# Spacing layer norm, a deeper ring of hidden tiles, phi written into the exp buffers, and a last block replicated on the matmul engine

## The chip, the cores and the metric

The kernel runs on one core of one Trainium2 chip. The metric is device time in microseconds (us) of that core, read as the median of several executions. Each execution also reports the mean granted clock of the matmul engine (1.00 is full speed), and one execution of each kernel was profiled. Engines are named as in the profile: PE (matmul; PEld is its weight load), ACT (ScalarE), DVE (VectorE), POOL (GpSimd), SP (which issues most of the DMAs).

## The reference

A transformer block in parallel form: the output is `x + attention(xn) + mlp(xn)`, with `xn = layernorm(x)`. There are 2048 tokens of width 512, 32 heads of 16, all bf16. Attention runs in four segments of 512 tokens. Each segment has causal softmax attention of its own, and reads a memory `M`, `z` that the segments before it have summed up.

```python
xn = _layernorm(x)
# attention, for each segment s of 512 tokens, each head (q, k, v = xn @ wq, wk, wv)
phi = lambda t: jnp.where(t > 0, t + 1.0, jnp.exp(t))
p = softmax(qs @ ks.T * scale + causal_mask)
a_dot = p @ vs
a_mem = (phi(qs) @ M) / (phi(qs) @ z + 1e-06)
o = g * a_mem + (1 - g) * a_dot          # g = sigmoid(beta), one number for each head
M = M + phi(ks).T @ vs
z = z + phi(ks).sum(0)
# ... all segments' o put together
return x + o @ wo + silu(xn @ w1) @ w2   # w1: 512 x 1792, w2: 1792 x 512
```

## The kernel before

The kernel keeps a feature-by-token layout. In each segment there are four blocks (`dt` 0 to 3) of eight heads, and each block has five score tiles of 128 x 2048. That makes 4 x 4 x 5 = 80 score tiles, and each is followed by one exp on ACT. These 80 exps are the beat of the program. All other work (projections, the MLP's 56 tiles of `w1` output, `w2`, `wo`, the memory) is cut into pieces that a small scheduler in the build places between score tiles. It keeps a virtual clock; `later(ns, fn)` emits `fn` once that clock has moved on by `ns`. The clock decides only the **order** of the instructions on each engine. The engines then run their lists in order and wait on semaphores.

Layer norm of a coming segment is done ahead, on DVE, in the gaps:

```python
HRING = 17                                     # w1 outputs that may wait for w2
ppool = ctx.enter_context(tc.tile_pool(name="ppool", bufs=8))      # Pt: exp outputs
hpool = ctx.enter_context(tc.tile_pool(name="hpool", bufs=HRING))  # hT: w1 outputs
work  = ctx.enter_context(tc.tile_pool(name="work",  bufs=2))

def ln_async(s):
    def step(j):                               # normalize tile j, transpose it by DMA
        xn_t = ln_norm(s, j)
        def move():
            nc.sync.dma_start_transpose(xnT[s][:, :, j * P : (j + 1) * P], xn_t[:])
            # ...
        later(700, move)
        if j < TPS - 1:
            later(1000, lambda: step(j + 1))
    def stats(half):                           # two tiles of statistics at once
        ln_stats(s, 2 * half)
        ln_stats(s, 2 * half + 1)
        ln_rstd(s, half)
        later(1500, lambda: stats(1) if half == 0 else free())
    # ... free() waits for the segment before last, then step(0)
    stats(0)

# where score tiles are emitted:
if (s, dt) == (0, 0):
    later(9000, lambda: ln_async(1))
elif dt == 1 and s + 2 < NSEG:
    ln_async(s + 2)
```

`phi(t)` is made as `max(t, 0) + min(exp(t), 1)`, with the exp on ACT, the min on POOL and the rest on DVE. For the keys the result goes to a tile `phiKT` (two buffers), and a DMA transposes it into `phiK`:

```python
def phi_part(src, dst, after, acc=None):
    ek = work.tile([P, L], BF16, name="ek")                    # two buffers
    nc.scalar.activation(out=ek[:], in_=src, func=AF.Exp)
    # ... mn() on POOL: ek = min(ek, 1); 800 ns later:
    def fin():
        nc.vector.scalar_tensor_tensor(out=dst, in0=src, scalar=0.0, in1=ek[:],
                                       op0=ALU.max, op1=ALU.add, accum_out=acc)
```

A `w1` tile is four matmuls on PE, a tanh on ACT, and a DVE pass that makes `hT`. At most `HRING` of them may be waiting for `w2`:

```python
while s not in ln_done or hcount["made"] - hcount["freed"] >= HRING:
    yield False
ps = gemm4(...)                                # 4 matmuls of 512 columns
nc.scalar.activation(out=th[:], in_=ps[:, :], func=AF.Tanh, scale=0.5)
# 700 ns later on DVE: hT = (th + 1) * ps
```

At the end of a segment, DVE takes the reciprocal of the softmax sums and of the memory's denominators. The result goes to DRAM and comes back broadcast, so that each head's number stands on its 16 partitions (`oT` and `Dr` hold it first, then are scaled in place):

```python
def scale(dt):
    nc.vector.tensor_tensor(out=oT[:, dt, :], in0=st["N_sb"][dt][:], in1=oT[:, dt, :], op=ALU.mult)
    if s > 0:
        nc.vector.tensor_tensor(out=Dr[:, dt, :], in0=st["phiQT"][:, dt, :], in1=Dr[:, dt, :], op=ALU.mult)
    later(1500, lambda: fin(dt))               # fin: psN = Mbf x Dr on PE, oT += psN on DVE
# ...
later((6500 if s < NSEG - 1 else 3000) + 1000 * (dt - d0), lambda dt=dt: scale(dt))
```

And the end of the program, after the last exp:

```python
for j in range(TPS):
    for ft in range(FA, FT):
        w2_part(st, j, psOs[j][:, :], range(ft, ft + 1), None)   # 28 w2 matmuls
        for g in list(due):
            pull(g)                            # norm_fill of the last segment
while st["normed"] < DT:
    ...
for j in range(TPS):
    wo_part(s, st, j, psOs[j][:, :])           # 16 wo matmuls, four for each j
```

The softmax here doesn't subtract the row's maximum and nothing guards it: scores larger than these inputs give would overflow.

## Time and profile before

| | before |
|---|---|
| median | 278.85 us (278.35 to 279.17, 4 runs) |
| profiled run: span from first to last instruction | 278.4 us |
| mean granted PE clock in that run | 0.969 |
| start of the first exp / start of the last exp | 14.3 us / 251.3 us |
| mean distance between exps | 3.0 us, for an exp of 1.88 us |

First, from the page of the kernel before: busy microseconds of each engine with the share of the span and the number of instructions; the clock granted to PE in 40 equal slices, in tenths of full speed; and the chain of work that ended last, by engine.

```profile
PE 235.1 (84%) x1908; PEld 100.7 (36%) x1908; DVE 170.5 (61%) x297; ACT 206.6 (74%) x192; POOL 127.9 (46%) x223
PEclk9999968999999997997999999999999999999979
PE 40%; DVE 22%; ACT 19%; issue 10%; POOL 4%; DMA 3%; ACTq 0%; DVEq 0%; SPq 0%
```

PE is the busiest engine and has the largest part of the chain, but only 40% of it. The chain changes hands all the time. A total says little in such a program; one has to ask, stretch by stretch, who is last.

The stretches used below are made from the exps. **Interval n** runs from the start of exp n to the start of exp n+1 (n counts from 0; read from ACT's timeline). The **tail** runs from the start of the last exp to the end. The next view, windows of the kernel before, gives five such stretches: intervals 5 and 6, 12 to 17, 24 to 36, 70 to 72, and the first 23.5 us of the tail. The columns are named in its first line; "x" counts instructions.

```profile
core 0: us, PE busy (x) PEld busy (x) DVE busy (x) ACT busy (x) POOL busy (x), PEclk, DMA share, GB/s
29.88:41.11 11.23, 5.90 (x56) 2.08 (x55) 11.02 (x25) 6.21 (x9) 7.37 (x16) 0.79 0.38 57
54.71:73.06 18.35, 15.64 (x127) 6.45 (x126) 13.73 (x22) 15.98 (x15) 13.60 (x21) 1.00 0.13 28
89.83:133.43 43.60, 34.14 (x290) 14.14 (x289) 30.18 (x53) 32.95 (x31) 28.25 (x45) 0.92 0.17 43
224.78:235.83 11.05, 7.18 (x70) 2.68 (x69) 9.39 (x19) 7.72 (x8) 2.91 (x5) 1.00 0.02 6
251.27:274.77 23.50, 19.03 (x104) 7.74 (x102) 14.17 (x24) 4.64 (x6) 1.64 (x2) 0.93 0.13 39
```

In the first line DVE is busy 11.02 of 11.23 us, while PE has 5.90 us of work: DVE alone sets that stretch, though it is the third engine by total. In the tail PE works 19.03 of 23.50 us, with a clock below 1.

DVE's timeline of the kernel before, from a little ahead of that first stretch, shows what fills it. (Left out between two statistics is the 0.18 us pass that gathers them.) Columns: start, duration, engine, line, operation, output and inputs, number; in brackets the idle time before, and what ended it.

```profile
24.68 0.66 DVE L134 BATCH_NORM_STATS2 stats<-x_sb 128x6 f32<-128x512 bf16 x1
...
28.71 0.69 DVE L226 SCALAR_TENSOR_TENSOR phiKT<-kT,ek 128x512 bf16<-128x512 bf16 x1 [3.15 <-DMA phiK<-phiKT]
...
29.33 0.69 DVE L134 BATCH_NORM_STATS2 stats<-x_sb 128x6 f32<-128x512 bf16 x1
...
30.15 0.66 DVE L134 BATCH_NORM_STATS2 stats<-x_sb 128x6 f32<-128x512 bf16 x1
...
30.95 0.66 DVE L302 CAST qT<-ps 128x512 bf16<-128x512 f32 x1
31.52 0.68 DVE L349 SCALAR_TENSOR_TENSOR hT<-th,ps 128x512 bf16<-128x512 bf16 x1
```

DVE stands idle for 3.15 us because `phiKT` has two buffers and the transposing DMA has not freed one. Then statistics come in pairs, and `qT` and `hT`, which PE and ACT need, stand behind them.

PE's timeline at the end of the kernel before:

```profile
264.30 4.05 PE L473 MATMUL psOt<-w_sb,hT 128*128 128x512 bf16 x11 [2.26 <-DVE hT L349]
...
268.57 2.56 PE L473 MATMUL psOt<-w_sb,hT 128*128 128x512 bf16 x11
270.96 0.38 PE L434 MATMUL psN<-Dr,Mbf 128*128 128x512 bf16 x1
271.18 3.93 PE L500 MATMUL psOt<-wo_sb,oT 128*128 128x512 bf16 x16
```

And DVE's in the same place:

```profile
261.51 1.75 DVE L667 RECIPROCAL rec<-zf 128x256 f32<-128x256 bf16 x1
263.29 0.35 DVE L668 TENSOR_SCALAR recg<-rec,gcol 128x256 bf16<-128x256 f32 x1
...
270.48 0.43 DVE L426 TENSOR_TENSOR Dr<-phiQT,Dr 128x512 bf16<-128x512 bf16 x1 [0.38 <-DMA Dr<-rec_d]
```

From the end of `recg` at 263.64 to the start of the last product with `Dr` at 270.48 it takes 6.84 us: one DMA to DRAM, two back. Only then can the last block's `psN` run, and all 16 `wo` matmuls come after it. Eleven `w2` matmuls take 4.05 us here, and eleven later ones 2.56 us: the first group started after an idle time of 2.26 us and ran at about half the clock.

### The profile page before, as it was taken

To read this page: it belongs to the slowest core of one execution; us is meant where nothing else is said; L and a number is where in the kernel's file an instruction comes from. 1 tells how busy PE (TensorE), PEld (TensorE's weight loads), DVE (VectorE), ACT (ScalarE), POOL (GpSimd) and SP (SyncE) were. 2 spreads that over 40 slices of the span, in tenths; PEclk is the share of its full clock that TensorE was granted. 3 is DMA by queue.
4 is the path that set the end of the run, shared out by engine and by line. 5 is a ranking of instruction groups with operands and counts; after the bars stand their busy time and mean duration, and the time that the engine had idled before them with its cause. 6 is when DMAs were issued, how large, how long until landed. Compare 5 with 4: busy or idle time off the path is not lost.

```text
span 278.4 us, 5105 instructions
## 1 busy us (share of the span) xinstructions
PE 235.1 (84%) x1908; PEld 100.7 (36%) x1908; DVE 170.5 (61%) x297; ACT 206.6 (74%) x192; POOL 127.9 (46%) x223
## 2 busy tenths in 40 slices
PE   7589569996989759796999988999999876998595
PEld 7433124432333333242344442343334322343241
DVE  4664895488656945974354749973436367457624
ACT  1499669888999887776799996887898986682300
POOL 3654653485724387585233555573343223423000
PEclk9999968999999997997999999999999999999979
DMA  6999141010112220103000440000100400131112
GB/s 210 380 358 221 38 62 29 3 30 19 28 22 51 48 77 12 38 11 76 26 26 11 86 154 11 8 5 27 62 13 17 144 13 14 45 117 34 33 49 75
DMA packets 29285, 18.69 MB, mean 67 GB/s; under 512 B 15180, under 2 KB 28748, under 8 KB 29260
## 3 DMA queue, kind: packets, MB, share of 16 engines
q1 hardware_dynamic: 29228, 18.35, 23.7%
q8 instruction: 15, 0.25, 0.3%
q14 instruction: 10, 0.08, 0.1%
q10 hardware_dynamic: 32, 0.01, 0.0%
HBM read 11.53 MB, written 2.49 MB: 50 GB/s over the span
## 4 chain that ended last, share of the span: by engine, by line
PE 40%; DVE 22%; ACT 19%; issue 10%; POOL 4%; DMA 3%; ACTq 0%; DVEq 0%; SPq 0%
ACT Pt L562 13%; PE ps L209 12%; PE psA L473 7%; PE psS L554 6%; DVE hT L349 5%; PE psO L473 5%; ACT th L343 4%; DVE stats L134 3%; PE psPV L629 3%; DVE rec L667 2%; PE psOt L473 2%; PE psO L500 2%; DMA phiK<-phiKT 2%; POOL Pt L574 2%; DVE phiKT L226 2%
## 5 line engine op out<-in xcount | busy, mean ns | idle before, releaser
L562 ACT ACTIVATE Pt<-psS 128x2048 bf16<-128x2048 f32 x80 | 150.3, 1879 | 20.8 <-PE psS L554 18.5
L574 POOL TENSOR_SCALAR_AFFINE_SELECT Pt<-Pt 128x512 bf16<-128x512 bf16 (+1 forms) x112 | 78.9, 718 | 97.6 <-ACT Pt L562 97.5
L209 PE MATMUL ps<-xnT,w_sb 128*128 128x512 bf16 x224 | 56.9, 388 | 5.3 <-DVE hT L349 3.2
L349 DVE SCALAR_TENSOR_TENSOR hT<-th,ps 128x512 bf16<-128x512 bf16 x56 | 37.3, 681 | 36.2 <-ACT th L343 35.7
L343 ACT ACTIVATE th<-ps 128x512 bf16<-128x512 f32 x56 | 32.6, 612 | 6.6 <-DVE hT L349 5.3
L209 PEld LDWEIGHTS <-w_sb 128*128 128x128 bf16 x224 | 20.6, 99 | 31.7 <-issue 13.0
L473 PEld LDWEIGHTS <-hT 128*128 128x128 bf16 x224 | 20.4, 100 | 32.2 <-issue 10.1
L473 PE MATMUL psA<-w_sb,hT 128*128 128x512 bf16 x112 | 28.9, 380 | 0.0
L554 PE MATMUL psS<-qT,kTo 32*128 32x512 bf16 (+3 forms) x256 | 17.6, 305 | 9.0 <-ACT Pt L562 7.7
L473 PE MATMUL psO<-w_sb,hT 128*128 128x512 bf16 x84 | 22.6, 395 | 0.0
L554 PE MATMUL psS<-qT,kT 16*128 16x512 bf16 (+3 forms) x256 | 17.6, 305 | 5.5 <-ACT Pt L562 5.3
L220 POOL TENSOR_SCALAR ek<-ek 128x512 bf16<-128x512 bf16 x24 | 16.1, 675 | 6.5 <-ACT ek L217 6.4
L509 DVE SCALAR_TENSOR_TENSOR o_t<-psO,acc 128x512 bf16<-128x512 f32 x12 | 8.3, 689 | 15.2 <-PE psO L500 15.1
L554 PEld LDWEIGHTS <-kTo 32*128 32x128 bf16 x256 | 6.7, 91 | 29.8 <-issue 28.4
L209 PE MATMUL ps<-xnT,wk_sb 128*128 128x512 bf16 x60 | 17.2, 390 | 0.1
L640 ACT CAST N_sb<-psPV 128x512 bf16<-128x512 f32 x16 | 9.4, 588 | 10.3 <-PE psPV L629 5.5
L209 PE MATMUL ps<-wv_sb,xnT 128*128 128x512 bf16 x64 | 15.8, 380 | 1.2 <-DVE V_109 L308 1.2
L209 PE MATMUL ps<-xnT,wq_sb 128*128 128x512 bf16 x60 | 16.8, 397 | 0.0
L488 DVE SCALAR_TENSOR_TENSOR acc<-psA,x_sb 128x512 f32<-128x512 f32 x16 | 11.0, 689 | 8.1 <-PE psA L473 8.1
L302 DVE CAST qT<-ps 128x512 bf16<-128x512 f32 x16 | 11.0, 685 | 7.1 <-PE ps L209 6.4
L629 PE MATMUL psPV<-Pt,V_109 128*32 128x512 bf16 (+3 forms) x256 | 11.1, 311 | 4.8 <-DVE hT L349 3.7
L638 DVE CAST No_t<-psPV 128x512 bf16<-128x512 f32 x16 | 11.0, 687 | 6.1 <-PE psPV L629 6.1
(82 smaller groups left out, 278.5 us busy)
## 6 DMA issues: line engine op xcount, KB each, us to landing
w_sb<-in_B_w_dram SPq DMA_DIRECT2D x2, 1792.0 KB
oT<-rec_d SPq DMA_DIRECT2D x16, 128.0 KB
out_dram<-o_t SPq DMA_DIRECT2D x12, 128.0 KB
Dr<-rec_d SPq DMA_DIRECT2D x12, 128.0 KB
x_sb<-in_A_x_dram SPq DMA_DIRECT2D x1, 1024.0 KB
N_sb<-No_t SPq DMA_DIRECT2D x64, 16.0 KB
x_sb<-in_A_x_dram SPq DMA_DIRECT2D x2, 256.0 KB
wk_sb<-in_A_wk_dram SPq DMA_DIRECT2D x1, 512.0 KB
```

What stands on the lines that cost most here:

```text
L209: nc.tensor.matmul(ps[:, :], lhsT=lhsTs(ki), rhs=rhss(ki), start=(ki == 0), stop=(ki == DT - 1))
L220: nc.gpsimd.tensor_scalar(out=ek[:], in0=ek[:], scalar1=1.0, scalar2=0.0, op0=ALU.min, op1=ALU.max)
L302: nc.vector.tensor_copy(out=qT[:], in_=ps[:, :])
L343: nc.scalar.activation(out=th[:], in_=ps[:, :], func=AF.Tanh, scale=0.5)
L349: nc.vector.scalar_tensor_tensor(out=hT[:], in0=th[:], scalar=1.0, in1=ps[:, :], op0=ALU.add, op1=ALU.mult)
L473: nc.tensor.matmul(psO, lhsT=st["hT"][ft][:, j * P : (j + 1) * P], rhs=w2_sb[:, ft, :], start=(ft in (0, FA)), stop=(ft == last),)
L488: nc.vector.scalar_tensor_tensor(out=acc[:], in0=psA[:, :], scalar=0.5, in1=x_sb[:, s * TPS + j, :], op0=ALU.mult, op1=ALU.add,)
L554: nc.tensor.matmul(psS[:, g, c : c + nq], lhsT=kk[r0:r1, kt * P : (kt + 1) * P], rhs=st["qT"][dt][r0:r1, kt * P : L], start=True, stop=Tru ...
L562: nc.scalar.activation(out=Pt[:], in_=psS[:], func=AF.Exp, scale=SCALE)
L574: nc.gpsimd.affine_select(out=v, in_=v, compare_op=ALU.is_ge, fill=0.0, base=0, pattern=[[0, v.shape[1]], [1, P]], channel_multiplier=-1,)
L629: nc.tensor.matmul(psPV[32 * g : 32 * g + 32, kt * P : L], lhsT=V[:, kt, 4 * dt + g, par : par + 2, :].rearrange("p r d -> p (r d)"), rhs= ...
L638: nc.vector.tensor_copy(out=dst[:], in_=psPV[:, :])
```

## The change

The intent, in four parts:

1. **LN**: layer-norm statistics come one tile at a time, 2 us apart (before: pairs, 1.5 us apart); normalized tiles 2 us apart (before: 1 us); segment 1 starts 2 us earlier, segments 2 and 3 one block later.
2. **phi**: the keys' phi goes back into its exp buffer `ek` (a ring of four); `phiKT` is gone. Freed memory goes to part 3.
3. **Ring**: 21 `w1` outputs may wait instead of 17; `Pt` has 7 buffers instead of 8.
4. **Tail**: for the last block the reciprocals are replicated over partitions by four matmuls with a selector matrix, not through DRAM; `oT` and `Dr` read the result in PSUM. The `wo` matmuls of the first three blocks go ahead of the last block's. The sums of the last block are issued from SP's queue, not ACT's.

```diff
-HRING = 17
+HRING = 21
-    ppool = ... name="ppool", bufs=8
+    ppool = ... name="ppool", bufs=7
@@ ln_async
-            later(700, move)
+            later(900, move)
-                later(1000, lambda: step(j + 1))
+                later(2000, lambda: step(j + 1))
-        def stats(half):
-            ln_stats(s, 2 * half)
-            ln_stats(s, 2 * half + 1)
-            ln_rstd(s, half)
-            later(1500, lambda: stats(1) if half == 0 else free())
+        def stats(j):
+            ln_stats(s, j)
+            if j % 2:
+                ln_rstd(s, j // 2)
+            later(2000, lambda: stats(j + 1) if j < TPS - 1 else free())
@@ where score tiles are emitted
-                later(9000, lambda: ln_async(1))
-            elif dt == 1 and s + 2 < NSEG:
+                later(7000, lambda: ln_async(1))
+            elif dt == 2 and s + 2 < NSEG:
@@ phi_part, k_tile
-        ek = work.tile([P, L], BF16, name="ek")
+        ek = work.tile([P, L], BF16, name="ek", bufs=4)
-                out=dst, in0=src, ...
+                out=ek[:] if dst is None else dst, in0=src, ...
-            phiKT = work.tile([P, L], BF16, name="phiKT")
-            def k_transposes():
+            def k_transposes(phiKT):
@@ norm_fill
-        def scale(dt):                 # oT first, then Dr, both in place
+        def scale(dt, R, D):           # Dr first, then oT, from R and D
+            if s == NSEG - 1 and dt == DT - 1:
+                reps = []
+                for w in (1, 0):
+                    ps = pp.tile([P, L], F32, name="psRep", tag="ps")
+                    for b in range(2):
+                        nc.tensor.matmul(ps[:, 256 * b : 256 * b + 256],
+                            lhsT=sel3[:, b, w, :], rhs=rec_d[:], start=True, stop=True)
+                    reps.append(ps)
+                scale(dt, reps[1][:, :], reps[0][:, :])
+                continue
@@ wo_part: takes the blocks to do; end of the program:
-    while st["normed"] < DT: ...
-    for j in range(TPS):
-        wo_part(s, st, j, psOs[j][:, :])
+    for n in (DT - 1, DT):
+        while st["normed"] < n: ...
+        for j in range(TPS):
+            wo_part(s, st, j, psOs[j][:, :], range(DT - 1) if n < DT else range(DT - 1, DT))
@@ pv_part: sums on SP's queue; recip returns before the DRAM write for the last block
-        q_sum = nc.scalar if last and dt == DT - 1 else nc.sync
+            if last and dt == DT - 1:
+                st["rec"][dt] = (recg, clock["vt"] + 1500)
+                return
```

(The build of the selector `sel3` from the identity matrix, on POOL, is left out.)

More of the change, by code (lines that the diff above doesn't have):

```diff
@@ L57 @@
     segp = ctx.enter_context(tc.tile_pool(name="segp", bufs=2))
-    ppool = ctx.enter_context(tc.tile_pool(name="ppool", bufs=8))
+    ppool = ctx.enter_context(tc.tile_pool(name="ppool", bufs=7))
     hpool = ctx.enter_context(tc.tile_pool(name="hpool", bufs=HRING))
@@ L226, in fin @@
             nc.vector.scalar_tensor_tensor(
-                out=dst, in0=src, scalar=0.0, in1=ek[:], op0=ALU.max, op1=ALU.add, accum_out=acc
+                out=ek[:] if dst is None else dst, in0=src, scalar=0.0, in1=ek[:],
+                op0=ALU.max, op1=ALU.add, accum_out=acc,
             )
             if after is not None:
-                later(1000, after)
+                later(1000, lambda: after(ek))
         later(900, mn)
@@ L292, in k_tile @@
                 lambda: phi_part(
-                    kT[:], phiKT[:], k_transposes, st["zc"][:, dt : dt + 1]
+                    kT[:], None, k_transposes, st["zc"][:, dt : dt + 1]
                 ),
@@ L419, in norm_fill @@
         st["normed"] = 0
-        def scale(dt):
-            nc.vector.tensor_tensor(
-                out=oT[:, dt, :], in0=st["N_sb"][dt][:], in1=oT[:, dt, :], op=ALU.mult
-            )
+        def scale(dt, R, D):
             if s > 0:
                 nc.vector.tensor_tensor(
-                    out=Dr[:, dt, :], in0=st["phiQT"][:, dt, :], in1=Dr[:, dt, :], op=ALU.mult
+                    out=Dr[:, dt, :], in0=st["phiQT"][:, dt, :], in1=D, op=ALU.mult
                 )
+            nc.vector.tensor_tensor(
+                out=oT[:, dt, :], in0=st["N_sb"][dt][:], in1=R, op=ALU.mult
+            )
             later(1500, lambda: fin(dt))
@@ L454, in norm_fill @@
             rec_d = st["rec"][dt][0]
+            if s == NSEG - 1 and dt == DT - 1:
[3 more added lines that the diff above has]
+                    for b in range(2):
+                        nc.tensor.matmul(
+                            ps[:, 256 * b : 256 * b + 256], lhsT=sel3[:, b, w, :], rhs=rec_d[:],
+                            start=True, stop=True,
+                        )
+                    reps.append(ps)
+                scale(dt, reps[1][:, :], reps[0][:, :])
+                continue
             for w, dst in ((0, oT), (1, Dr))[:nw]:
@@ L462, in norm_fill @@
                 )
-            later((6500 if s < NSEG - 1 else 3000) + 1000 * (dt - d0), lambda dt=dt: scale(dt))
+            later((6500 if s < NSEG - 1 else 3000) + 1000 * (dt - d0), lambda dt=dt: scale(dt, oT[:, dt, :], Dr[:, dt, :]))
         while st["normed"] < DT:
@@ L495, in first_fill, with wo_part @@
         st["first_done"] = True
-    def wo_part(s, st, j, psO):
+    def wo_part(s, st, j, psO, dts=range(DT)):
         t = s * TPS + j
-        for dt in range(DT):
+        for dt in dts:
             nc.tensor.matmul(
@@ L504, in wo_part @@
             pe(215)
+        if dts[-1] < DT - 1:
+            return
         if s == NSEG - 1:
@@ L646, in sums @@
                     z0 = 16 * (1 - par)
-                    q_sum.dma_start(
+                    nc.sync.dma_start(
                         out=zf[r : r + 7 : 2, :],
@@ L671, in recip @@
             d0 = max(st["rec"], default=-1) + 1
+            if last and dt == DT - 1:
+                st["rec"][dt] = (recg, clock["vt"] + 1500)
+                return
             rec_d = dpool.tile([2, H, 2, 256], BF16, name="rec_d")
@@ L739 @@
     later(20000, gate)
+    sel3 = cpool.tile([P, 2, 2, P], BF16, name="sel3")
+    nc.gpsimd.tensor_copy(
+        out=sel3[:, :, :, :].rearrange("p b w (h d) -> p (b w) h d", d=DH),
+        in_=ident[:, :]
+        .rearrange("p (r h) -> p r h", r=4)[:, :, 24:32]
+        .unsqueeze(3)
+        .broadcast_to([P, 4, 8, DH]),
+    )
     bmask = cpool.tile([P, P], BF16, name="bmask")
@@ L874 @@
                 pull(g)
-    while st["normed"] < DT:
-        for g in list(due):
-            pull(g)
-        clock["vt"] += 200
-        run_due()
-    for j in range(TPS):
-        wo_part(s, st, j, psOs[j][:, :])
+    for n in (DT - 1, DT):
+        while st["normed"] < n:
+            for g in list(due):
+                pull(g)
+            clock["vt"] += 200
+            run_due()
+        for j in range(TPS):
+            wo_part(s, st, j, psOs[j][:, :], range(DT - 1) if n < DT else range(DT - 1, DT))
     clock["vt"] += 5000
```

## The prediction

> **What bounds the kernel now.** The busy table shows PE 235.1 of 278.4 us (84%), ACT 206.6, DVE 170.5; the chain of waits is PE 40%, DVE 22%, ACT 19%. No single engine bounds it. The 80 exps of score tiles (1.88 us each) start at 14.3 to 251.3 us, 3.0 us apart. For each interval I took the larger of PE's work (0.217 us per 512-column matmul) and ACT's (1.76 us per exp, 0.6 per other pass). This estimate sums to 213 us against 237 measured; most intervals match within 0.2 us. The excess sits in few places (timeline):
> - 29.9 to 41.1 us: two intervals of 5.9 and 5.3 us, 5.3 too long. DVE waited 3.1 us for a transpose to free a phiK buffer, then did layer-norm statistics (0.66+0.18 us each) in pairs while hT evictions, and PE, stood behind.
> - 57 to 68: ACT waits for DVE to free exp buffers, 1.7.
> - 89.8 to 133.4: 43.6 us for 13 intervals, about 9 too long. Statistics delay hT; the w1 ring is full, so PE has 0.9 to 1.1 us of work in two intervals; then its clock is half (matmuls at 0.43 us) as the projections start; an exp waits 1.4 us for a buffer.
> - 168 to 176 and 225 to 233: attention scaling on DVE, 5.5.
> - After the last exp (ends 253.2): 25.2 us. The sums go out on ACT's queue, delaying N's copy by 1.5 us; the reciprocal ends at 263.3; the round trip through DRAM lets Dr's product finish only at 270.9; PE's clock halves from 264.3 to 268.3; all 16 wo matmuls follow (271.2 to 275.1).
>
> **What the change does** (instruction order compared).
> 1. Layer norm: no work removed; statistics come one at a time, 2 us apart; segments 2 and 3 start a block later. phi goes back into the exp buffer (ring of 4), so DVE no longer waits for the first transposes. Segment 3's statistics and norms (3.2+1.6 us) fall into its projection burst, where DVE has about 21 us of work in 19 us: part is given back.
> 2. Ring 21: sixteen more w1 matmuls run where PE was empty; one nearly empty interval remains instead of two; two w1 tiles instead of four are left for the tail.
> 3. Seven Pt buffers: PV frees the oldest in time; about 0.
> 4. Tail: one rec write and two broadcasts vanish (263.7 to 270.5); four 256-column matmuls come in. Dr and oT read PSUM: 0.42 becomes 0.69 us, as other PSUM passes here; the Trainium skill, "VectorE: DVE Perf Modes", "Why PSUM operands drop a tier", agrees. 12 wo matmuls run before the last block is ready. PE's work becomes the limit (estimate 15 us after PV); sums wait behind earlier broadcasts, so the reciprocal gains about 1 us.
>
> **On the critical path (estimates):** startup -4; phi buffers -1.5; 90 to 133 us -3.5; 225 to 233 us -1; elsewhere -0.5; tail -2.5. Sum -13.
>
> **Predicted: 266.0 us, 80% range 261 to 272.** Faster by over 2%: 0.88; within 2%: 0.11; slower: 0.01.
>
> **Right or wrong in the profile:** the two long startup intervals fall to about 3.5 each, DVE's 3.1 us wait gone; the 13 intervals take about 40 us; no exp waits over 1 us for a phi buffer; last exp to end about 22.5 us, 12 wo matmuls before the last oT.
>
> **What would make it wrong:** exp buffers waiting for transposes, stalling ACT; DVE's burst in segment 1 costing more; PE idling before the replication, its clock halving anyway (0.217 to 0.43 us after gaps here).

## The result and the profile after

| | before | after |
|---|---|---|
| median | 278.85 us (278.35 to 279.17, 4 runs) | 271.14 us (270.24 to 272.39, 4 runs) |
| profiled span | 278.4 us | 270.7 us |
| mean granted clock in the profiled run | 0.969 | 0.974 |

The ratio is 0.9728, with a 95% interval of 0.9676 to 0.978: faster. Ratios here are the mean time of one kernel's fast runs over the mean of the other's fast runs of the same rounds, so they are not quite the ratio of the medians quoted. Executions over 1.5% slower than the fastest of the same kernel are left out of the means.

The four runs after are not alike: 272.39 us at clock 0.974, 272.02 at 0.981, 270.24 and 270.26 at 0.993. The same program is granted a different clock from run to run, and the profiled run is the slowest of the four. So differences below 1 us between two profiles are not to be leaned on.

From the page of the changed kernel, the same three lines:

```profile
PE 229.3 (85%) x1879; PEld 100.9 (37%) x1912; DVE 170.9 (63%) x297; ACT 206.0 (76%) x192; POOL 128.5 (47%) x224
PEclk9869999999999999999999999999999995999999
PE 39%; ACT 22%; DVE 18%; issue 11%; POOL 5%; DMA 3%; DVEq 0%; SPq 0%; ACTq 0%; POOLq 0%
```

The work is the same (DVE 170.5 to 170.9 us, ACT 206.6 to 206.0). What fell is time in which the last engine was waited for. New marks stand in the clock: a 5 in a slice near 227 us, and an 8 and a 6 between 7 and 20 us. Windows give a clock of 0.87 up to the first exp and 0.92 in intervals 0 to 4, where the kernel before had 1.00 in both.

Windows of the changed kernel, the same five stretches (intervals 5 and 6, 12 to 17, 24 to 36, 70 to 72, and 23.5 us of the tail):

```profile
31.41:37.53 6.12, 4.47 (x55) 2.01 (x55) 5.49 (x12) 5.79 (x9) 4.17 (x10) 1.00 0.31 46
50.93:69.32 18.39, 15.27 (x124) 6.42 (x126) 14.60 (x25) 15.92 (x16) 14.86 (x23) 1.00 0.14 28
86.09:126.30 40.21, 31.19 (x283) 13.86 (x288) 32.18 (x59) 34.32 (x34) 26.06 (x43) 1.00 0.21 48
216.39:230.32 13.93, 10.43 (x73) 3.69 (x74) 10.08 (x19) 8.91 (x10) 2.98 (x5) 0.75 0.04 10
245.73:269.23 23.50, 17.04 (x102) 7.26 (x102) 15.64 (x26) 3.66 (x4) 1.93 (x3) 1.00 0.13 43
```

Stretch by stretch, the two profiles differ as follows. The parts add up to the whole (278.4 to 270.7 is 7.7 less).

| stretch | before | after | difference | predicted |
|---|---|---|---|---|
| up to exp 0, and intervals 0 to 4 | 29.88 | 31.41 | +1.53 | 0 |
| intervals 5 and 6 (startup) | 11.23 | 6.12 | -5.11 | -4 |
| intervals 12 to 17 (phi buffers) | 18.35 | 18.39 | +0.04 | -1.5 |
| intervals 24 to 36 | 43.60 | 40.21 | -3.39 | -3.5 |
| intervals 67 to 72 | 20.18 | 21.84 | +1.66 | -1 |
| tail | 27.13 | 24.97 | -2.16 | -2.5 |
| all other intervals | 128.0 | 127.8 | -0.27 | -0.5 |

DVE's timeline of the changed kernel at the startup stretch:

```profile
25.40 0.68 DVE L134 BATCH_NORM_STATS2 stats<-x_sb 128x6 f32<-128x512 bf16 x1
...
26.22 0.66 DVE L227 SCALAR_TENSOR_TENSOR ek<-kT,ek 128x512 bf16<-128x512 bf16 x1
...
26.80 0.69 DVE L302 CAST qT<-ps 128x512 bf16<-128x512 f32 x1
27.41 0.68 DVE L134 BATCH_NORM_STATS2 stats<-x_sb 128x6 f32<-128x512 bf16 x1
```

The wait for the transpose is gone, and one pass of statistics stands between the others where there were two. DVE's load in the window falls from 25 instructions to 12: three more run earlier (20 in intervals 0 to 4, where there were 17), and the rest come after a window that is itself 5 us shorter.

PE's timeline at the end of the changed kernel:

```profile
252.94 3.04 PE L485 MATMUL psOt<-w_sb,hT 128*128 128x512 bf16 x12
257.99 0.61 PE L460 MATMUL psRep<-recg,sel_286 128*128 128x256 bf16 x4 [2.00 <-DVE recg L681]
...
260.17 2.32 PE L485 MATMUL psOt<-w_sb,hT 128*128 128x512 bf16 x10
262.32 3.71 PE L512 MATMUL psOt<-wo_sb,oT 128*128 128x512 bf16 x15
```

And DVE's:

```profile
255.79 1.75 DVE L680 RECIPROCAL rec<-zf 128x256 f32<-128x256 bf16 x1 [1.33 <-DMA zf<-N_sb]
257.58 0.35 DVE L681 TENSOR_SCALAR recg<-rec,gcol 128x256 bf16<-128x256 f32 x1
258.52 0.68 DVE L423 TENSOR_TENSOR Dr<-phiQT,psRep 128x512 bf16<-128x512 bf16 x1
261.49 0.69 DVE L426 TENSOR_TENSOR oT<-N_sb,psRep 128x512 bf16<-128x512 bf16 x1 [2.29 <-DMA N_sb<-No_t]
```

Replication takes 0.61 us where the way through DRAM took 6.84. The first product that needs it starts 0.59 us after `recg` ends (257.93 to 258.52). The price is visible too: these two passes read PSUM and take 0.68 and 0.69 us, against 0.43 before. PE then runs without a gap to the end of its work, at full clock. What did not move is the last reciprocal: it starts 10.06 us after the last exp's start, and 10.24 before.

### The profile page after: what moved, and what is told of

Read it like the earlier page. It is cut to its first block, busy times and chain, and to the rows that moved or that the text cites. A ratio compares the mean times of both kernels' runs of the same rounds, so it can differ in the third digit from the quotient of the medians.

```text
span 270.7 us, 5102 instructions
## 1 busy us (share of the span) xinstructions
PE 229.3 (85%) x1879; PEld 100.9 (37%) x1912; DVE 170.9 (63%) x297; ACT 206.0 (76%) x192; POOL 128.5 (47%) x224
## 4 chain that ended last, share of the span: by engine, by line
PE 39%; ACT 22%; DVE 18%; issue 11%; POOL 5%; DMA 3%; DVEq 0%; SPq 0%; ACTq 0%; POOLq 0%
ACT Pt L576 14%; PE ps L209 13%; PE psA L485 6%; PE psS L568 6%; ACT th L343 4%; PE psO L485 4%; DVE hT L349 4%; PE psO L512 2%; POOL Pt L588 2%; DVE stats L134 2%; DVE oT L426 2%; DVE Dr L423 1%; DVE rec L680 1%; PE psOt L485 1%; PE psPV L642 1%
## 5 line engine op out<-in xcount | busy, mean ns | idle before, releaser
L209 PE MATMUL ps<-xnT,w_sb 128*128 128x512 bf16 x211 | 55.7, 388 | 4.7 <-DVE hT L349 2.8
L485 PE MATMUL psO<-w_sb,hT 128*128 128x512 bf16 x82 | 21.4, 381 | 0.0
L221 POOL TENSOR_SCALAR ek<-ek 128x512 bf16<-128x512 bf16 x24 | 14.9, 629 | 5.1 <-ACT ek L218 5.0
L209 PE MATMUL ps<-xnT,wk_sb 128*128 128x512 bf16 x54 | 16.4, 395 | 0.5 <-issue 0.2
L209 PE MATMUL ps<-xnT,wq_sb 128*128 128x512 bf16 x57 | 15.9, 392 | 0.3
L568 PEld LDWEIGHTS <-kT 16*128 16x128 bf16 x256 | 6.3, 92 | 19.9 <-issue 19.8
## 6 DMA issues: line engine op xcount, KB each, us to landing
oT<-rec_d SPq DMA_DIRECT2D x15, 128.0 KB
out_dram<-o_t SPq DMA_DIRECT2D x12, 128.0 KB
Dr<-rec_d SPq DMA_DIRECT2D x11, 128.0 KB
```

Of the source, the lines that this page charges most:

```text
L209: nc.tensor.matmul(ps[:, :], lhsT=lhsTs(ki), rhs=rhss(ki), start=(ki == 0), stop=(ki == DT - 1))
L221: nc.gpsimd.tensor_scalar(out=ek[:], in0=ek[:], scalar1=1.0, scalar2=0.0, op0=ALU.min, op1=ALU.max)
L485: nc.tensor.matmul(psO, lhsT=st["hT"][ft][:, j * P : (j + 1) * P], rhs=w2_sb[:, ft, :], start=(ft in (0, FA)), stop=(ft == last),)
L568: nc.tensor.matmul(psS[:, g, c : c + nq], lhsT=kk[r0:r1, kt * P : (kt + 1) * P], rhs=st["qT"][dt][r0:r1, kt * P : L], start=True, stop=Tru ...
```

## The experiments

Kernels of one group ran on the same chip, six runs each, interleaved with the kernel before. Its median was 278.84 us for the first four, 279.74 for the next four and 280.02 for the last four. Because it moves from chip to chip, ratios are compared across groups, not microseconds. The fast runs of the kernel before scatter by 2.6 to 3.9 us within a group, so half a point between ratios of two groups is not to be leaned on. The profiles are single runs. Letters for theories are local to each run. The questions were:

- **Startup**: was it the wait for the transpose (phi), or the spacing of the statistics (LN)?
- **Intervals 24 to 36**: is it the deeper ring, as predicted, or the other parts?
- **Intervals 67 to 72**: why slower?
- **Tail**: does the new end give its gain alone?

### The changed kernel again

No edit.

> The changed kernel once more, unaltered. Its four runs fell into two pairs (272.0 and 272.4 us at a mean granted clock of 0.974 to 0.981; 270.2 and 270.3 us at 0.993). Theory A: the 2 us between the pairs is PE's clock, which halves or does not halve in two places (before the first exp, and at about 223 to 229 us), by luck of the phase; then the runs scatter again over 270 to 272.5, and each run's time goes with its mean clock. Rival: something else differs (DMA); then time and clock do not go together.

Measured: 271.2 us (270.24 to 272.9), ratio 0.9751 [0.9709, 0.9794]. Again the clock goes with the time: 270.24 us at 0.992, 270.68 and 270.88 at 0.986, 272.48 at 0.975, though 272.9 came at 0.98. The profile's span is 268.9 us. Its first exp and intervals 0 to 4 take 30.14 us, against 31.41 in the profile above and 29.88 before, so most of the loss at the start was of that run. The stretch 67 to 72 is slow again (21.42 us), so that loss is of the program.

### The changed kernel with the old ring

```diff
-HRING = 21
+HRING = 17
-    ppool = ... name="ppool", bufs=7
+    ppool = ... name="ppool", bufs=8
```

> The changed kernel with the w1 ring back at 17 and Pt buffers at 8. Theory A (the ring filled intervals 27 and 28 and took work from the tail): slower than the changed kernel by 1 to 3 us, with two or three intervals of near-empty PE at 95 to 105 us and more PE work after the last exp. Theory B (the ring only moved work: its extra w1 tiles in the intervals 70 to 72 cost there, and it lets segment 3's norms run into the projection burst, what it gave elsewhere): within 1 us of the changed kernel.

Measured: 271.38 us (270.43 to 272.43), ratio 0.9741 [0.9705, 0.9777]: the same as with the ring. Intervals 24 to 36 take 39.49 us, no longer than with the ring (40.21, 40.22). A window of this kernel over these intervals, in the columns of the windows above:

```profile
86.13:125.62 39.49, 31.05 (x274) 13.41 (x278) 27.16 (x51) 32.57 (x30) 28.07 (x44) 0.87 0.17 41
```

The ring was not what shortened them. (The seven `Pt` buffers were always changed along with the ring, so this tests the pair.) In the profile two effects oppose each other: intervals 67 to 72 are 2.3 us shorter than with the ring (19.09 against 21.42 in the run above), and the tail is 3.35 us longer (28.22 against 24.87), longer even than before (27.13). Intervals 12 to 17 are 1.2 us longer as well, but there the clock differs: over all profiles they take 18.1 to 18.6 us at clock 1.00 (nine profiles) and 19.45 to 19.70 at 0.91 (five, this one among them).

### The changed kernel with the old layer-norm timing

```diff
-            later(2000, lambda: stats(j + 1) if j < TPS - 1 else free())   # one tile each
+            later(1500, lambda: stats(1) if half == 0 else free())        # two tiles each
-                later(2000, lambda: step(j + 1))
+                later(1000, lambda: step(j + 1))
-                later(7000, lambda: ln_async(1))
-            elif dt == 2 and s + 2 < NSEG:
+                later(9000, lambda: ln_async(1))
+            elif dt == 1 and s + 2 < NSEG:
```

> The changed kernel with the layer norm's timing of before (pairs of statistics, start a block earlier). Theory A (the 5.1 us gained in intervals 5 and 6 come from the phi buffers, and spreading the statistics gave 1 to 2 us there but cost 3 to 4 us in segment 1's projections, intervals 30 to 36): as fast as the changed kernel or up to 2 us faster. Rival B (the spreading is what gained at startup): slower by 3 us or more, intervals 5 and 6 back at 10 us or more together.

Measured: 276.01 us (272.97 to 278.49), ratio 0.9836 [0.9786, 0.9886]. Three of the six runs (274.46, 272.97 and 273.99) count as fast; the other three, over 277 us, as slow, and no claim rests on those. 0.85 points of the 2.5 go, but the two ratios' intervals just overlap, so the total alone does not settle it. A window of this kernel over intervals 5 and 6 shows where; its columns are those of the windows above.

```profile
30.03:39.27 9.24, 5.14 (x55) 2.02 (x55) 9.10 (x20) 6.10 (x9) 6.56 (x14) 0.89 0.25 48
```

DVE is full again, 9.10 of 9.24 us, although no pass waits for a transpose here. The window, 3.1 us longer than the changed kernel's, answers the startup question.

### The changed kernel with the old phi buffers

```diff
-        ek = work.tile([P, L], BF16, name="ek", bufs=4)
+        ek = work.tile([P, L], BF16, name="ek")
-                out=ek[:] if dst is None else dst, ...
+                out=dst, ...
+            phiKT = work.tile([P, L], BF16, name="phiKT")
```

> The changed kernel with the separate two-buffer phi tile and the two exp buffers of before. Theory A (the transposes held DVE at startup): DVE's wait of about 3 us before phi returns at 25 to 29 us, intervals 5 and 6 together lengthen by 3 us or more, total plus 3 to 4 us. Rival B (spreading the statistics is what mattered): intervals 5 and 6 stay below 7.5 us together and the total moves less than 1.5 us. In intervals 12 to 17 both say no change in the sum (18.4 us), for I now think DVE's work bounds it there.

Measured: 271.13 us (270.26 to 272.32), ratio 0.9744 [0.9706, 0.9782]: no loss in total. In the profile DVE waits 3.97 us for the transpose, longer than the 3.15 of before, and yet intervals 5 and 6 grow by only 1.0 us, to 7.11. Intervals 12 to 17, where the phi buffers were to bring 1.5 us, take 18.62, against 18.39 with the new buffers. Windows of this kernel, over intervals 5 and 6 and over 70 to 72:

```profile
30.07:37.18 7.11, 4.69 (x55) 1.97 (x55) 6.53 (x15) 6.00 (x9) 4.43 (x11) 1.00 0.31 59
216.85:228.65 11.80, 7.95 (x74) 3.18 (x75) 9.62 (x19) 8.67 (x11) 2.98 (x5) 1.00 0.04 8
```

The second line matters for intervals 70 to 72. PE's order is the same there as in the changed kernel, and the stretch takes 11.80 us at clock 1.00, not 13.93 at 0.75. The difference of 2 us goes with the clock, which halved in one of these runs and not in the other. Over all eight profiles with the deeper ring and the scaling 1 us apart, these intervals take 13.51 to 13.93 us at a clock of 0.75 (three), 13.09 to 13.20 at 0.87 (three), and 11.80 at 1.00 (two: this one and the run with segment 3's layer norm earlier).

### The changed kernel with the old ending

```diff
-                scale(dt, reps[1][:, :], reps[0][:, :])    # replication on PE: taken out
-    for n in (DT - 1, DT): ...                             # wo in two steps: taken out
+    while st["normed"] < DT: ...
+    for j in range(TPS):
+        wo_part(s, st, j, psOs[j][:, :])
+        q_sum = nc.scalar if last and dt == DT - 1 else nc.sync
```

> The changed kernel with the end of before (the last block's reciprocals through DRAM, sums on ACT's queue, all wo matmuls last). In the changed kernel 24.9 us pass from the start of the last exp to the end. Theory A (replication on PE and wo in two parts are worth the 2.5 us that I predicted, over and above the two w1 tiles that the ring took out of the tail): the tail lengthens by 2.5 us or more, to 27.4 or more, the total to about 274. Rival B (the tail's gain was the two w1 tiles that left it, for without the larger ring it was 3.3 us longer): the tail stays within 1 us of 24.9.

Measured: 277.38 us (275.36 to 279.49), ratio 0.9893 [0.9836, 0.995]. The ending is worth 1.4 points (0.9893 to 0.9751), more than the 2.16 us read from the two profiles (0.8%). Its profile fell in a slow run (279.49), so its size is not used, only its pattern: the tail takes 31.56 us, longer than the 27.13 of before. In this profile the old ending with the new ring is worse than the old ending with the old ring; the run with the ring alone, below, shows the same. The pieces of the new ending (replication, early `wo`, the queue of the sums) were not run one by one.

### All w2 matmuls ahead of the replication

The changed kernel lets PE idle for 2.00 us in front of the replication, with `w2` matmuls standing behind it. This run puts them in front.

```diff
             if s == NSEG - 1 and dt == DT - 1:
+                while not st.get("w2_all"):
+                    yield
                 reps = []
...
+    st["w2_all"] = True                        # after the loop over the w2 matmuls
+    for g in list(due):
+        pull(g)
```

> The changed kernel, but PE replicates the reciprocals only after all 28 w2 matmuls of the last tiles instead of after 12. In the changed kernel PE stands idle 2.0 us before the replication (it waits for the reciprocal with 16 w2 matmuls, 3.5 us of work, still ahead), and then works to the end without a gap. Theory A (PE's order bounds the tail): the tail shortens by about 2 us, to about 22.9. Rival B (the reciprocal, its DRAM-free chain on DVE and the merge of N bound it, which ends at 261.5): it shortens by less than 0.7 us.

Measured: 270.16 us (269.31 to 271.07), ratio 0.9654 [0.9614, 0.9695]; the tail is 24.15 us in place of 24.87. That lies between what the theories gave. (The ratio is a whole point better than the changed kernel's, which is more than 0.7 us of tail; the medians, of two groups, differ by 1.0 us.) PE's timeline of this kernel shows why not all of the idle time came back:

```profile
252.47 4.12 PE L487 MATMUL psOt<-w_sb,hT 128*128 128x512 bf16 x17
257.84 0.39 PE L434 MATMUL psN<-Dr,Mbf 128*128 128x512 bf16 x1 [1.25 <-DVE Dr L423]
258.07 2.54 PE L487 MATMUL psOt<-w_sb,hT 128*128 128x512 bf16 x11
260.44 0.60 PE L462 MATMUL psRep<-recg,sel 128*128 128x256 bf16 x4
```

The gap in front of the replication is gone, but a new one of 1.25 us stands further ahead: block 2's `psN` waits for DVE, where the scaling of `Dr` is queued behind the reciprocal.

### Segment 3's layer norm one block earlier again

In the changed kernel the norm work of segment 3 falls into the projections of segment 2, where I had counted about 21 us of DVE work in 19. This run keeps the spacing but starts segment 3 at block 1.

```diff
-            elif dt == 2 and s + 2 < NSEG:
+            elif dt == 2 - s and s + 2 < NSEG:
```

> The changed kernel, but segment 3's layer norm starts at the second block of segment 1, as before, still spread. Its statistics then come among the w1 evictions at 90 to 100 us, not in the projection burst. Theory A (the burst on DVE costs what I called given back): intervals 24 to 36 shorten from 40.2 to 38 us or less, total about minus 2. Rival B (DVE has the same work in the 13 intervals either way): within 0.7 us of 40.2.

Measured: 271.76 us (270.63 to 273.7), ratio 0.9716 [0.967, 0.9762]: the same. Intervals 24 to 36 take 39.44 us in place of 40.21, less than the burst was held to cost. The single long interval stays long (4.82 us for interval 33, where the changed kernel has 4.94 for interval 32), and intervals 37 to 66 grow from 82.2 to 83.48 us. Moving the same DVE work by one block moved the long interval and saved nothing overall.

### Segment 2's attention scaling spread out

In intervals 70 to 72 DVE does the scaling of segment 2 (twelve passes for four blocks) between the `hT` passes. PE's timeline of the changed kernel there:

```profile
219.55 0.38 PE L434 MATMUL psN<-Dr,Mbf 128*128 128x512 bf16 x1 [0.86 <-DVE hT L349]
...
224.65 0.59 PE L434 MATMUL psN<-Dr,Mbf 128*128 128x512 bf16 x1 [0.70 <-DVE oT L438]
...
226.96 2.70 PE L209 MATMUL ps<-xnT,w_sb 128*128 128x512 bf16 x6 [0.22 <-issue]
```

PE waits for DVE again and again (waits of 0.56, 0.54 and 0.22 us lie in the part left out), and from about 222.7 us its clock is half: a single matmul takes 0.59 in place of 0.38 us, and six take 2.70. Behind this point stand two `w1` tiles (eight matmuls, seven of them recorded from 225.71 us on) that the kernel before ran in intervals 67 to 69. The edit moves the scalings apart:

```diff
-            later((6500 if s < NSEG - 1 else 3000) + 1000 * (dt - d0), ...)
+            later((6500 if s < NSEG - 1 else 3000) + (1800 if s == NSEG - 2 else 1000) * (dt - d0), ...)
```

> The changed kernel with segment 2's attention scaling 1.8 us apart instead of 1.0. In the changed kernel intervals 70 to 72 take 13.5 to 13.9 us with PE's clock at half for half of it, and 11.8 in a run at full clock (without the phi buffers). Theory A (the scaling on DVE and the w1 evictions share 9.5 us of DVE time there, PE starves and its clock falls): intervals 70 to 73 (16.5 us in the profile of the changed kernel) shorten by 2 us or more and the clock stays full. Rival B (the clock falls by chance of its window): the clock is still at half in some profiles and the time moves by less than 1 us.

Measured: 267.65 us (265.81 to 268.55), ratio 0.9554 [0.9505, 0.9602], at clocks of 0.985 to 0.999. This is 2.0 points better than the changed kernel (0.9751), and 4.1 us better than the run above, of the same group. Windows of this kernel over intervals 70 to 72, and then PE's timeline:

```profile
215.48:226.03 10.55, 8.11 (x75) 2.96 (x74) 9.76 (x19) 8.65 (x10) 2.98 (x5) 1.00 0.04 10
```

```profile
226.08 1.46 PE L209 MATMUL ps<-xnT,w_sb 128*128 128x512 bf16 x6
```

The same DVE work (9.76 against 10.08 us) and PE work fit into 10.55 us at full clock; six `w1` matmuls take 1.46 us. Intervals 67 to 72 fall from 21.84 and 21.42 us in the two profiles of the changed kernel to 18.46. That is the term with the largest error in the prediction, and one number in the program's order removes it. Of the 3 us, about 2 are the clock; against the two profiles at full clock (11.80 us for intervals 70 to 72) the spread is 1.25 us shorter. Both profiles with the spread (this one and the combination below) have a clock of 1.00 there, against two of eight without it; that is few, so that the spread keeps the clock is likely and not proved. Other spacings were not run.

### The kernel before with the layer-norm timing alone

```diff
-HRING kept at 17, phi, ring and ending as before
+ln_async and its start as in the change
```

> The kernel before with the layer norm's new timing alone. Theory A (the timing of the statistics made most of the gain in intervals 24 to 36 and at startup; the phi buffers and the ring, taken away one at a time, brought none of it back): intervals 5 and 6 at about 7.1 us together (11.2 before), intervals 24 to 36 at about 40 us (43.6 before), total about minus 5 us, to 273 or 274. Rival B (the ring, as I predicted, made the gain at 24 to 36): 43 us there, total minus 4 at the most.

Measured: 274.48 us (272.94 to 277.3, one of the six runs slow, at 277.3), ratio 0.9811 [0.9759, 0.9862]. Intervals 5 and 6 fall from 11.23 to 8.41 us, intervals 24 to 36 from 43.60 to 39.94. Here interval 5 stays long (6.05 us), because DVE waits 4.53 us for the transpose just ahead of it, and interval 6 is mended (5.32 to 2.36). Its tail, with ring and ending as before, takes 28.61 us, 1.5 more than in the kernel before.

### The kernel before with the ring alone

```diff
-HRING = 17
+HRING = 21
-    ppool = ... name="ppool", bufs=8
+    ppool = ... name="ppool", bufs=7
```

> The kernel before with the ring of 21 and seven Pt buffers alone. Theory A (the ring moves work and gains next to nothing): within 1.5 us of the kernel before, intervals 24 to 36 no shorter than 42 us, the tail shorter by 1 to 2 us and the intervals 67 to 72 longer. Rival B (the ring fills PE's empty intervals, minus 3 us at 24 to 36): 40 to 41 us there and a total of minus 3 us or more.

Measured: 283.39 us (280.08 to 287.17), ratio 1.0095 [1.003, 1.0161]: alone, the deeper ring does not help; by the interval it costs 0.3 to 1.6%. The profiled run is a slow one (285.0; another was 287.17), so again only its pattern is used. Neither theory held: intervals 24 to 36 did shorten, to 40.70 us, but the total did not, and the tail, which was to get shorter, got longer by 4.2 us. PE's timeline of it at the end:

```profile
266.02 2.53 PE L473 MATMUL psOt<-w_sb,hT 128*128 128x512 bf16 x11
273.20 0.61 PE L434 MATMUL psN<-Dr,Mbf 128*128 128x512 bf16 x1 [4.64 <-DVE Dr L426]
273.60 6.38 PE L500 MATMUL psOt<-wo_sb,oT 128*128 128x512 bf16 x16
```

With fewer `w1` tiles left for the tail, PE has nothing to do during the way through DRAM. It idles for 4.64 us, and its 16 last matmuls take 6.38 us where the kernel before took 3.93. The old-ending run had the same picture (4.78 us of idle time, then 6.31 us). In these two profiles, work moved out of a stretch that waits for DMAs was not saved; it had been cover. How much it costs in a fast run is not shown. Intervals 37 to 66 are 3 us longer in this profile as well; that is not explained, and may be the slow run.

### The kernel before with the phi buffers alone

```diff
-phiKT as the destination of the keys' phi, two ek buffers
+phi back into ek, four ek buffers; all else as before
```

> The kernel before with phi written back into the exp buffer alone. If the two startup causes overlap: intervals 5 and 6 shorten from 11.2 to about 9.2 us (the changed kernel without the layer norm's timing showed 9.2), 12 to 17 stay at 18.4 (or 19.6 where PE's clock is at half), and the total moves by minus 1.5 to minus 2.5 us. If the phi buffers bound nothing else, no other group of intervals moves by more than its clock explains.

Measured: 276.03 us (275.45 to 280.88, two of the six runs slow at 280.8), ratio 0.9867 [0.9817, 0.9917]. Intervals 5 and 6 fall from 11.23 to 9.55 us. It is the mirror image of the run with the layer norm alone: interval 5 is mended (5.91 to 4.22) and interval 6 is not (5.32 to 5.33). Intervals 12 to 17 hardly move (18.35 to 18.10).

### A combination

The changed kernel with the scaling spread out, the `w2` matmuls in front of the replication, and the last segment's scaling emitted earlier (so that `Dr` stands ahead of the reciprocal on DVE).

```diff
-            later((6500 if s < NSEG - 1 else 3000) + 1000 * (dt - d0), ...)
+            later((6500 if s < NSEG - 1 else 1500) + (1800 if s in (2,) else 1000) * (dt - d0), ...)
+                while not st.get("w2_all"):      # and the rest as in the run above
+                    yield
```

> The changed kernel with segment 2's scaling 1.8 us apart, the replication after all w2 matmuls, and the third block's scaling issued 1.5 us earlier, so that DVE does it before the last reciprocal and PE's matmul for it does not stand in front of the w2 matmuls. Spreading alone measured minus 3.5 us, the replication's place alone about minus 1, with 1.25 us of PE's idle time left that the third part should remove. If the three are independent: 265 to 266 us, ratio about 0.95, tail about 23 us. If the shorter tail only waits for the merge of N instead: about 267 us.

Measured: 267.65 us (266.26 to 268.29), ratio 0.957 [0.9523, 0.9618]. It beats both kernels, but it misses the total expected of it: it is not better than the spread alone (0.9554). The tail did what was meant: 23.85 us, the shortest of all, with no idle gap on PE from 250.8 us on. In this profile the first exp starts at 15.57 us, in that of the spread alone at 13.44, and the spans are 266.0 and 266.3. From the first exp to the end they take 250.4 and 252.9 us: 1.0 us of the difference is the tail, and 1.3 are intervals 12 to 17, where the clock was 0.91 in the spread's run. A start 2 us later and the clock can hide a gain of 1 us between two groups; that they do is not shown.

## Why the prediction was right or wrong

The class and the range were right: 271.14 us lies in 261 to 272, near its upper end, and partly by luck: one large term had the right size for a wrong reason. The point, 266.0, was 5.1 us too low. In terms of the sum of -13, of which the profile shows -7.7:

**Startup (-4; measured -5.1): right in kind, undersized.** The two long intervals were to fall to about 3.5 each; they fell to 3.69 and 2.43. Both causes named there are real, but they are not of equal weight. Taking the layer-norm spacing away costs 3.1 us (9.24 against 6.12), taking the phi buffers away 1.0 (7.11). Alone they give 2.8 and 1.7. After the result I held the phi buffers for the main cause, because DVE's idle time of 3.15 us is the most striking line; the run with the old phi buffers refuted that. There DVE idles for 3.97 us and only 1 us of it is lost; I read this as room that the single passes of statistics leave DVE to catch up.

**Phi buffers in 57 to 68 us (-1.5; measured 0): wrong.** The failed step is "ACT waits for DVE to free exp buffers, 1.7". The wait was real and it went away; another took its place. On ACT's timeline, the wait in the kernel before is this:

```profile
61.13 0.63 ACT L217 ACTIVATE ek<-qT 128x512 bf16<-128x512 bf16 x1 [1.02 <-DVE phiQT L226]
```

and in the changed kernel this:

```profile
62.90 0.63 ACT L218 ACTIVATE ek<-kT 128x512 bf16<-128x512 bf16 x1 [1.50 <-DVE kT L271]
```

With more buffers ACT reaches the next exp sooner and then waits for the copy of `kT`, made by the same DVE. Interval 13 fell from 3.93 to 3.14 us, and interval 15 rose from 3.64 to 4.45. Here the buffer wait showed who was late; it was not a sum that more buffers gave back. That DVE's queue is what binds here is read from these two waits; no run lightened DVE in this stretch, so it is argued and not shown.

**90 to 133 us (-3.5; measured -3.4): right size, wrong reason.** The prediction gave the gain to the ring ("sixteen more w1 matmuls run where PE was empty"). With the old ring the gain is all there (39.49 us). It is also there without the new layer norm (39.78) or, for the most part, without the new phi buffers (40.89). Each of the three parts alone brings the 43.60 us down (layer norm 39.94, ring 40.70, phi buffers 41.27; single profiles, and the ring's is of a slow run). In these profiles the pile-up needed all three old settings at once, and any one change undoes most of it. Such gains must not be added up by part.

**225 to 233 us (-1; measured +1.7, and +1.2 in the second profile): wrong, the largest error.** These figures are for intervals 67 to 72; in 70 to 72 alone, which is the stretch that the prediction named, the loss is 2.9 us (11.05 to 13.93), and intervals 67 to 69 gain 1.2 (9.13 to 7.91). Seven or eight `w1` matmuls have moved from there into interval 72, behind a crowd of DVE passes (10.08 of 13.93 us in intervals 70 to 72). That move by itself is not the loss: with the old ring and the new layer norm they stand there too, and intervals 70 to 72 take 11.15 us at clock 1.00. With the deeper ring they take 11.80 at full clock, and 13.1 to 13.9 where the clock fell. The prediction gave no reason for its -1; the step that failed is that the scaling's cost on DVE would shrink here. PE still idles for half a microsecond at a time, and in this profile its clock is halved. With the old ring the six intervals take 19.09 us; with the scaling spread out and the ring kept, 18.46.

**Tail (-2.5; measured -2.2): right, but not of the ending alone.** "About 22.5 us", counted from the end of the last exp, became 23.1 (24.97 less 1.88). The replication and the early `wo` matmuls work as described. "The reciprocal gains about 1 us" failed: it gained 0.2 (10.24 to 10.06 us from the last exp's start). I had not seen that the ring and the ending need each other: new ending with old ring 28.22 us, both old 27.13, both new 24.97 (and the ring with the old ending over 31, in slow runs). The layer norm has a part in it: with its new timing and both old, the tail takes 28.61, so like against like the new ending alone gives 0.4 us, and ring and ending together 3.6. One counter-sign named in the prediction came true: PE idled for 2.00 us in front of the replication. The other did not, since the clock stayed at 1.00 there. The cost of reading PSUM was predicted exactly: 0.69 us. The Trainium skill, "VectorE: DVE Perf Modes", section "Why PSUM operands drop a tier", says that "any PSUM operand caps you at 2×_1P max (and 1× for fp32)", and the replicated tiles are fp32 in PSUM. The trace agrees: 0.43 us before, 0.68 and 0.69 us after, on the same shape.

**The start (0; measured +1.5)** goes with the clock; the changed kernel shows both states: over all profiles the first exp starts at 13.44 to 14.56 us where the clock up to it was 1.00 (nine profiles; the changed kernel's second one is among them, at 14.56), and at 15.08 to 15.64 where it was 0.87 to 0.89 (five).

**The clock.** The Trainium skill, "TensorE: Matmul & The Clock Gate", Part 1 ("The HAM clock gate"), says that PE's clock is halved when a freely running window of about 3.4 us finds it idle, and that the moment therefore differs from run to run. The traces agree (but for the idle window, see the last section) with the two speeds (six matmuls of 512 columns in 1.46 or 2.70 us) and with the scatter: 270.24 us at a mean clock of 0.993 and 272.39 at 0.974 for one program. In the list of what could go wrong, the halving stood at the replication; it came at 222.7 us instead.

Still open: which runs get the halving in intervals 70 to 72. Two profiles of the changed kernel had it, and those with the old phi buffers and with segment 3's layer norm earlier, with the same order on PE there, did not. The kernel before did not have it either, though PE was busy for only 7.18 of 11.05 us there. So idle time on PE alone does not settle it.

## What to carry to other kernels

Before you credit a part of a change with a gain, run the change without that part and the part alone: here one stretch's gain could be had from any of three parts, one part (the ring) was worth nothing or less by itself, and two parts (ring and ending) paid far more together than alone. When a buffer takes a wait away, look whether the engine that was late has less to do: here the wait came back at its next result (1.02 us before, 1.50 after). Think twice before moving work out of a tail that waits for DMAs: it may be cover. And try spreading DVE passes that come in bursts, even when their sum fits: here that took 3 us off six intervals, about 2 of which go with PE's clock.

## What the Trainium skill lacked or had wrong

- "TensorE: Matmul & The Clock Gate", Part 1, "What's actually happening": it names an idle window of about 3.4 us as the cause of the half clock, but not how busy a window may be and still count as idle. In two places here the clock was halved with no idle time longer than 2.3 us: in the kernel before, 2.26 us in front of 264.30 (PE busy 1.30 of the 4 us before 264); in the changed kernel, PE busy 2.07 of 4 us before 222, with gaps of at most 0.9 us. The busy share of 4 us alone does not decide it: in the run with the old phi buffers PE was busy 1.83 of 4 us (221 to 225), with a gap of 1.23 us, and the clock stayed at 1.00. The section "A second HAM failure mode: psum-queue depth-cycling" speaks of short idle times in words, without a limit.
- "VectorE: DVE Perf Modes", "First, the fixed hardware budget": it says how a reciprocal is made, without its cost. The traces show 1.75 us for 128 x 256, bf16 to f32, where a multiplication of the same size takes 0.35 us. On this kernel's tail that is the longest single DVE pass.
- "DMA: Bandwidth & Descriptors", "Anatomy of one DMA": its fit (about 2.0 us fixed) is measured for DMAs issued from GpSimd. The ones here were issued from SP. The write of 64 KB was issued at 263.68 us, the read that had to wait for it at 266.86, so 3.2 us for the first; with two reads of 128 KB behind it, issued one after the other, the whole way through DRAM took 6.84 us. No page that I read sets the other way beside it: replication over partitions by matmul with a selector, which took 0.61 us for the same two tiles.
